# One branch for both halves of the first layer in the last group of a mixture of experts, the second layer behind it

## The chip, the core and the metric

The kernel runs on one core of a Trainium2 chip. A core has a matrix engine (TensorE, PE in the profile, with its weight loads as PEld), three engines for elementwise work (VectorE or DVE, ScalarE or ACT, GpSimd or POOL) and SyncE (SP), which issues DMA transfers. Each engine has its own instruction queue and waits for the others by semaphores. The metric is the time of the whole program on the device in microseconds, lower is better. Each time is the median of several runs.

## The reference

The reference is attention in a linear form with random features (8 batches, 8 heads, sequence 576, head size 64, 128 features), whose output becomes 4608 tokens of 512 numbers, and on them a mixture of experts in which each token goes to one of 8 experts. Cut to what matters here:

```python
q_p, k_p = (phi(q_s), phi(k_s))                 # 128 random features, exp
num = np.einsum('bhsm,bhmd->bhsd', q_p, kv)     # kv = sum over s of k_p * v
x = (num / den).transpose(0, 2, 1, 3).reshape(4608, 512)

e_idx = np.argmax(x @ w_gate, axis=1)           # one expert per token
gate_w = probs[np.arange(N), e_idx]
eom = 1.0 / (1.0 + np.exp(-(x @ w_output_gate)))
for e in range(8):
    mask = e_idx == e
    h = np.maximum(x[mask] @ w1[e], 0.0)        # 512 -> 1024
    ye = h @ w2[e]                              # 1024 -> 512
    out[mask] = gate_w[mask, None] * eom[mask, e, None] * ye
```

Inputs and outputs are float32.

## The kernel before

**Stages.** Attention runs as 32 units in four chunks of the tokens. Its output goes to a DRAM array (`rows`), token by token, and after each chunk a routing step counts the tokens of each expert. The expert work is cut into *items*: an item is up to 128 tokens of one expert. Items come in four groups of 8, 8, 9 and 24 slots, one group behind each chunk (`KS`); the last group holds whatever tokens are left, and its later slots stay empty. How many tokens an item has, which expert it uses, and whether the expert differs from that of the item before are known only at run time. They are read into registers of the engines, and the code of a step stands in `tc.If` branches on these registers: `regs[n, 0, ...]` says whether item n exists, `regs[n, 1, ...]` whether it begins a new expert, and in the last group `regs[n, "few", ...]` whether it has at most 64 tokens (`FEW`, half of `P` = 128).

**One item.** GpSimd gathers the token rows by an indirect DMA (`gx`), SyncE issues a DMA that transposes them (`xt`). All products are taken in fp16 as three terms of high and low parts (high by high, high by low, low by high). The first layer (`hidden`, L1373) runs in two halves of 512 hidden numbers: each half is 48 matmuls of 128x128 weights on the tokens into one PSUM bank (`ph`), with as many tokens as columns: 128 in the full arm, 64 in the small one. For each half ScalarE takes the relu (`relu`, L1388, into `hh`, the fp16 high part), then VectorE the remainder (`rest`, L1392, into `hl`); in the small arm two memsets follow that clear the unused lanes (L1397, L1398). The second layer (`second`, L1400) has for each half 12 matmuls with 512 columns, from `hh` and `hl` with the weights `w2h` and `w2l`, and both halves sum into one bank (`po`). ScalarE scales the result (`os`, L1456), and GpSimd scatters it to the output (`put`, L1445).

**A new expert.** SyncE loads its weights in float32 (`bring`, L1289). Each of the two layers' weights is split by quarters: ScalarE makes the fp16 high part (`swh`, L365), VectorE the low part (`swl`, L369), so eight splits on each of the two engines for one switch, inside a branch that is empty when the expert stays. A quarter of the new weights may be written only when TensorE has used the old one: `free` at L1333 names the step behind which this is so.

**What sets the order.** The order on each engine is fixed when the program is built. A planner (`Plan.order`, L173) lists all steps with their engine, an assumed duration, the steps that they come after, and a rank. It goes through time, and of the steps that can start within 0.1 us of the earliest (`TIE`) takes the one with the lowest rank. An expert switch counts with its full duration (0.95 us for a split on ScalarE, 1.14 on VectorE) only behind the items after which one is assumed (`ASSUMED`, in the last group items 26, 31 and 37), otherwise with 0.1. `early` makes a step count as done before its end, `lead` lets a step start that long before another one is done, or, if it is negative, that long after. PSUM's banks are given out there too: three banks (class `b`) are shared by the `ph` and `po` of all items.

**The steps that the change touches.** In the first three groups an item has four steps on TensorE: `hA` and `hB` (the two halves of the first layer) and two steps `out`. In the last group (`joint`) before the change it has three: `hA`, a branch with the first half; `hB`, one branch with the second half and the first part of the second layer (`hidden_and_second`); and `out` 1, the second part of the second layer, outside of the branch on the number of tokens. `either` (L1360) makes that branch: `tc.If` on `few` with the 64-token code first, `Else` with the 128-token code. ScalarE's relu and VectorE's remainder go through `either` too. In this run 38 items were executed; those of the last group are 25 to 37, and 25, 36 and 37 have at most 64 tokens.

Of the kernel before, what the change touches and what calls it, by code (L numbers as in the profile page):

```python
# [21 lines left out]
P = 128  # L22
# [3 lines left out]
DM = H * D  # L26
# [7 lines left out]
FC = F // P  # L34
# [15 lines left out]
NG = len(GROUPS)  # L50
# [206 lines left out]
def attention_moe(ctx: ExitStack, tc: tile.TileContext, kqt, kqn, v, om, wg, w1, w2, cf, cm, ci, out):  # L257
# [1009 lines left out]
    def item(n):  # L1267
# [45 lines left out]
        for w in (1, 2):  # L1313

            user = n - 1 if n <= ALT else n - 2
            before = cuts_of(user, w) if n != ALT and user >= 0 else []
            plan.add(
                ("bring", n, w), ("SP",), 1.8 if full and aside(n) else 0.4, lambda w=w: bring(w), rank=-900.0 + n,
                after=[flag_step[n, 1, ("SP",)]] + behind(n, w) + (before if n else [("w0l", w, x) for x in range(NQ)] if SPECULATE else []), dma=5.8 if full else 0.0,
                tiles=[b for b, _ in SPARE[w]] if n == ALT else [],  # L1320
            )
            if gr < FINE:
                last = [] if n == 0 else [("hB", n - 1)] if w == 1 else [("out", n - 1, 1)]
                plan.add(
                    ("sw", n, w), ("ACT", "DVE"), (3.8, 4.9) if full else (0.3, 0.3), lambda w=w: switch(w), rank=-1500.0 + n,
                    early=2.2 if full else None,
                    after=[flag_step[n, 1, ("ACT", "DVE")], ("bring", n, w)] + last,
                )
                continue
            for x in range(NQ):  # L1330
                half = x // (NQ // 2)
                joint = FEW > 0 and slots[n - 1][0] == NG - 1
                free = ("hB" if half else "hA", n - 1) if w == 1 else ("hB", n - 1) if joint and not half else ("out", n - 1, half)  # L1333
                plan.add(
                    ("swh", n, w, x), ("ACT",), 0.95 if full else 0.1, lambda w=w, x=x: cut(w, x, "ACT"),
                    after=[flag_step[n, 1, ("ACT",)], ("bring", n, w), free], rank=CUT + n,
                )
                plan.add(
                    ("swl", n, w, x), ("DVE",), 1.14 if full else 0.1, lambda w=w, x=x: cut(w, x, "DVE"),
                    after=[flag_step[n, 1, ("DVE",)], ("swh", n, w, x)], rank=CUT + n,  # L1340
                )
# [18 lines left out]
        def either(eng, fn):  # L1360

            if gr < NG - 1 or not FEW:
                return lambda: fn(P)

            def step():
                with tc.If(regs[n, "few", (eng,)] > 0) as small_block:
                    fn(FEW)
                with small_block.Else():
                    fn(P)

            return step

        def hidden(g, w_):  # L1373
# [16 lines left out]
        def rest(g, w_):  # L1390
# [5 lines left out]
            if w_ < P:  # L1396
                nc.vector.memset(hh(n)[:, sl, w_:], 0.0)  # L1397
                nc.vector.memset(hl(n)[:, sl, w_:], 0.0)  # L1398

        def second(g):  # L1400
            po = banks["po", n]
            for f in range(g * (FC // 2), (g + 1) * (FC // 2)):
# [2 lines left out]
                        po, x(n)[:, f, :], w[f // 2][:, f % 2, :], start=(f == 0 and a == 0), stop=(f == FC - 1 and a == 2)  # L1405
                    )


        joint = gr == NG - 1 and FEW > 0

        def hidden_and_second(w_):
            hidden(1, w_)
            second(0)

        for g in range(2):
            name = "hA" if g == 0 else "hB"
            both = joint and g
            add(
                (name, n), "PE", 5.2 if both else 2.6,
                either("PE", hidden_and_second if both else lambda w_, g=g: hidden(g, w_)),  # L1420
                tiles=[("xt", n), ("hh", n), ("hl", n)] if both else [("xt", n)],
                bank=[("b", ("ph", n, g), [FC // 2, P])] + ([("b", ("po", n), [DM])] if both else []),
                after=[("xt", n), *cuts_of(n, 1, halves_of[g])]
                + ([("hA", n)] if g else [("hB", n - 1)] if joint and slots[n - 1][0] == gr else [])
                + ([("rest", n, 0), *cuts_of(n, 2, halves_of[0])] if both else []),
                **(dict(early=2.6, lead={("rest", n, 0): 2.6, **{c: 2.6 for c in cuts_of(n, 2, halves_of[0])}}) if both else {}),
            )
            add(
                ("relu", n, g), "ACT", 0.48, either("ACT", lambda w_, g=g: relu(g, w_)), after=[(name, n)], rank=-600.0 + n,
                tiles=[("hh", n)],  # L1430
            )
            add(
                ("rest", n, g), "DVE", 0.6, either("DVE", lambda w_, g=g: rest(g, w_)), after=[("relu", n, g)], rank=-600.0 + n,
                tiles=[("hh", n), ("hl", n)], frees=[("ph", n, g)],
            )

        for g in range(1 if joint else 0, 2):
            add(
                ("out", n, g), "PE", 2.6, lambda g=g: second(g), rank=R + 5, tiles=[("hh", n), ("hl", n)],
                after=[("rest", n, g), *cuts_of(n, 2, halves_of[g])] + ([("hB" if joint else "out", n, *(() if joint else (0,)))] if g else []),  # L1440
                bank=None if g else ("b", ("po", n), [DM]),
            )

# [97 lines left out]
```

## Time and profile before

| what | value |
|---|---|
| runs | 699.62, 702.99, 706.42 us (median 702.99) |
| the profiled execution's own time | 703.85 us |
| its span, first to last instruction | 702.1 us |
| mean granted TensorE clock | 0.951 |
| busy TensorE matmuls, of the span | 615.9 us (88%) |
| busy VectorE, ScalarE, GpSimd | 472.8, 372.0, 330.2 us |
| last group's matmuls | 552.1 to 689.2, 137.1 us |
| TensorE busy in them | 132.4 us, at a granted clock of 1.00 |
| from the last matmul's stretch to the end | 12.9 us |

The profile is of one execution, so stretches of it are set against its own 703.85 us, and not against the median. A row of a timeline is the start in us from the beginning of the span, the duration, the engine, the source line, the operation, output and input with their shapes, and in square brackets how long the engine had been idle and what ended that. Rows of TensorE show a matmul longer than the distance to the next one, since matmuls overlap. A row with `PEldq COMPARE_BRANCH` lists branch instructions in TensorE's queue: their count, their least, median and greatest duration in ns, and when the first and the last began.

### The profile page before, as it was taken

The page shows a single profiled execution, that of the slowest core. Times are in us where ns is not written, and L with a number is a line of the kernel's source. Part 1 is how long each engine was busy: PE and PEld are TensorE (multiplying, and loading weights), DVE is VectorE, ACT ScalarE, POOL GpSimd, SP SyncE. Part 2 cuts the span into 40 slices and gives each one's busy share as a digit, 9 for nine tenths or more (in the row PEclk, how much of TensorE's full clock was granted, in tenths as well). Part 3 has the DMA queues.
Part 4 walks back from the last instruction along what each step waited for, and adds up shares of the span by engine and source line. Part 5 has one row for each costly group of instructions (what it writes and reads, how often), then busy time and mean ns, then how long its engine had stood idle before and what let it go on. Part 6 is the DMA issues. An engine that isn't in the chain of part 4 may idle for free. (4 is left out here: it accounts for less than half of the span.)

```text
span 702.1 us, 22897 instructions
## 1 busy us (share of the span) xinstructions
PE 615.9 (88%) x8763; PEld 474.6 (68%) x8763; DVE 472.8 (67%) x1300; ACT 372.0 (53%) x869; POOL 330.2 (47%) x207
## 2 busy tenths in 40 slices
PE   6999974899989987989989877899999999999982
PEld 6889863766766765766767646677777576676751
DVE  5997888977797897778899977763465431341160
ACT  5967883776586546666866425652341431331150
POOL 1323353668757857858489546666121121131210
PEclk9999986899999998999999967989999999999997
DMA  8565887999999939798899584639864934722730
GB/s 295 213 153 162 277 243 204 205 271 250 300 251 299 266 95 249 207 266 284 226 280 214 125 195 95 110 74 212 298 154 118 263 87 133 265 78 66 255 104 8
DMA packets 181031, 137.76 MB, mean 196 GB/s; under 512 B 139535, under 2 KB 162575, under 8 KB 179600
## 3 DMA queue, kind: packets, MB, share of 16 engines
q1 hardware_dynamic: 174800, 116.13, 65.0%
q0 software_dynamic: 6080, 19.72, 8.3%
q8 instruction: 83, 1.36, 0.8%
q14 instruction: 68, 0.56, 0.3%
HBM read 83.69 MB, written 19.69 MB: 147 GB/s over the span
## 5 line engine op out<-in xcount | busy, mean ns | idle before, releaser
L544 ACT ACTIVATE ef<-pp,nb 128x128 f32<-128x128 f32 x576 | 164.2, 388 | 118.8 <-DVE nb L538 87.5
L1381 PE MATMUL ph<-xt,w1h 128*128 128x128 f16 (+1 forms) x2432 | 209.4, 220 | 3.1 <-DMA xt<-gx 2.3
L1381 PE MATMUL ph<-xt,w1l 128*128 128x128 f16 (+1 forms) x1216 | 205.1, 220 | 1.1 <-DVE w1l L369 0.6
L1381 PEld LDWEIGHTS <-w1h 128*128 128x128 f16 x2432 | 184.2, 99 | 12.1 <-issue 3.0
L1392 DVE SCALAR_TENSOR_TENSOR hl<-ph,hh 128x512 f16<-128x512 f32 (+1 forms) x76 | 50.4, 665 | 123.3 <-ACTq L1310 78.7
L567 POOL TENSOR_TENSOR es<-ef,es 128x1152 f16<-128x1152 f32 x44 | 106.2, 2416 | 49.7 <-ACT es L565 28.2
L1381 PEld LDWEIGHTS <-w1l 128*128 128x128 f16 x1216 | 120.1, 100 | 0.9 <-DVE w1l L369 0.8
L1404 PE MATMUL po<-w2h,hh 128*128 128x512 f16 x304 | 116.4, 383 | 3.8 <-DVE hl L1398 2.1
L1404 PE MATMUL po<-w2h,hl 128*128 128x512 f16 x304 | 116.2, 382 | 1.0 <-DVE hl L1392 0.8
L1404 PE MATMUL po<-w2l,hh 128*128 128x512 f16 x304 | 116.2, 382 | 0.0
L1344 POOL DMA_INDIRECT gx<-rows,gi x38 | 40.9, 1076 | 153.6 <-ACT os L1456 108.6
L525 DVE TENSOR_REDUCE pp<-pp 128x3 f32<-128x384 f32 x192 | 102.1, 555 | 10.8 <-PE pp L503 9.8
L1404 PEld LDWEIGHTS <-hh 128*128 128x128 f16 x608 | 55.7, 98 | 67.6 <-issue 5.4
L1388 ACT ACTIVATE hh<-ph 128x512 f16<-128x512 f32 (+1 forms) x76 | 44.3, 585 | 93.7 <-PE ph L1381 88.4
L503 PE MATMUL pp<-omh,xhi 64*128 64x128 f16 x432 | 49.2, 232 | 28.0 <-ACT ef L544 9.8
L437 POOL TENSOR_TENSOR xlo<-xt,xhi 128x1152 f16<-128x1152 f32 x24 | 57.2, 2382 | 30.8 <-ACT xhi L430 8.3
L715 POOL TENSOR_TENSOR xs<-xf,xs 128x576 f16<-128x576 f32 x32 | 42.8, 1337 | 57.2 <-DVE xs L711 25.8
L503 PEld LDWEIGHTS <-xhi 64*128 64x128 f16 x864 | 37.9, 101 | 43.2 <-issue 18.0
L1456 ACT ACTIVATE os<-po,gx 128x512 f32<-128x512 f32 x38 | 26.1, 688 | 76.8 <-PE po L1404 63.9
L565 ACT CAST es<-ef 128x1152 f16<-128x1152 f32 x44 | 51.2, 1172 | 9.3 <-DMA et<-es 8.7
L1404 PEld LDWEIGHTS <-hl 128*128 128x128 f16 x304 | 29.9, 98 | 38.6 <-DVE hl L1392 2.4
L681 PE MATMUL pn<-kvs,et 128*128 128x65 f16 (+1 forms) x960 | 41.8, 199 | 11.6 <-DMA et<-es 5.9
(160 smaller groups left out, 1015.8 us busy)
## 6 DMA issues: line engine op xcount, KB each, us to landing
r<-w SPq DMA_DIRECT2D x10, 2048.0 KB
xt<-kqt SPq DMA_DIRECT2D x32, 576.0 KB
xn<-kqn SPq DMA_DIRECT2D x24, 576.0 KB
rawv<-v SPq DMA_DIRECT2D x32, 325.0 KB
rows<-xs SPq DMA_DIRECT2D x16, 576.0 KB
r<-w SPq DMA_DIRECT2D x8, 512.0 KB
ef<-w SPq DMA_DIRECT2D x2, 512.0 KB
et<-w SPq DMA_DIRECT2D x2, 512.0 KB
```

The source lines that it names most:

```text
L437: lambda t0=t0, t1=t1: nc.gpsimd.tensor_tensor(out=xl(u)[:, t0:t1], in0=xt32(u)[:, t0:t1], in1=xh(u)[:, t0:t1], op=ALU.subtract),
L503: nc.tensor.matmul(banks["pp", 2 * u + i, g][:, c, :], x[r, t], w[r, :], start=(a == 0), stop=(a == len(ops) - 1))
L525: nc.vector.tensor_reduce(out=pp[:, 3, 0:3], in_=pp[:, 0:3, :], op=ALU.min, axis=AX.X)
L544: nc.scalar.activation(ef(n)[:, c, :], banks["pp", n, g][:, c % 3, :], AF.Exp, bias=nb(n)[:, c : c + 1], scale=-SK)
L565: nc.scalar.copy(es(slot_es(n))[:, 0], ef(n))
L567: nc.gpsimd.tensor_tensor(out=es(slot_es(n))[:, 1], in0=ef(n), in1=es(slot_es(n))[:, 0], op=ALU.subtract)
L681: nc.tensor.matmul(pn[lo:hi, c - c0, :], a[:, c, lo:hi], w[:, b, :], start=(i == 0), stop=(i == len(ops) - 1))
L715: nc.gpsimd.tensor_tensor(out=x[:, :, P + o : P + o + D], in0=xf(pr)[:, :, o : o + D], in1=x[:, :, o : o + D], op=ALU.subtract)
L1381: nc.tensor.matmul(ph[:, f4, 0:w_], w[qd][:, kk, fo : fo + P], xt(n)[:, x, 0:w_], start=(a == 0), stop=(a == 3 * KC - 1))
L1388: nc.scalar.activation(hh(n)[:, sl, 0:w_], banks["ph", n, g][:, :, 0:w_], AF.Relu)
L1392: nc.vector.scalar_tensor_tensor(out=hl(n)[:, sl, 0:w_], in0=banks["ph", n, g][:, :, 0:w_], scalar=0.0, in1=hh(n)[:, sl, 0:w_], op0=ALU.ma ...
L1404: nc.tensor.matmul(po, x(n)[:, f, :], w[f // 2][:, f % 2, :], start=(f == 0 and a == 0), stop=(f == FC - 1 and a == 2))
```

## The change

In the last group the step `hA` is gone. One step `hB` now holds both halves of the first layer (`hidden_both`) in one branch, and on TensorE this branch has the 128-token code first and the 64-token code in the `Else` (`step_full_first`, on `few < 1`). ScalarE's and VectorE's branches stay as they were. The second layer's two parts are both steps `out` outside of the branch, as in the other groups.

For the planner the joint step costs 5.2 us and counts as done after 2.6 (`early`); the first relu comes after that, the second 2.6 us later (`lead` of -2.6). The joint step takes both `ph` banks at once and the first `out` takes `po`; before, `hA` took one `ph`, and `hB` took the other together with `po`. Quarters of the first layer's weights that belong to the second half may come 2.6 us later than the step's start. All four splits of a new expert's first-layer weights now wait for the joint step of the item before, where the first two waited for `hA`; the first two of the second layer wait for `out` 0, where they waited for `hB`. The three groups ahead are built as before.

```diff
--- before.py
+++ after.py
@@ -1330,7 +1330,7 @@
             for x in range(NQ):
                 half = x // (NQ // 2)
                 joint = FEW > 0 and slots[n - 1][0] == NG - 1
-                free = ("hB" if half else "hA", n - 1) if w == 1 else ("hB", n - 1) if joint and not half else ("out", n - 1, half)
+                free = ("hB" if half or joint else "hA", n - 1) if w == 1 else ("out", n - 1, half)
                 plan.add(
                     ("swh", n, w, x), ("ACT",), 0.95 if full else 0.1, lambda w=w, x=x: cut(w, x, "ACT"),
                     after=[flag_step[n, 1, ("ACT",)], ("bring", n, w), free], rank=CUT + n,
@@ -1367,6 +1367,15 @@
                     fn(FEW)
                 with small_block.Else():
                     fn(P)
+
+            def step_full_first():
+                with tc.If(regs[n, "few", (eng,)] < 1) as full_block:
+                    fn(P)
+                with full_block.Else():
+                    fn(FEW)
+
+            if eng == "PE":
+                return step_full_first
 
             return step
 
@@ -1397,6 +1406,37 @@
                 nc.vector.memset(hh(n)[:, sl, w_:], 0.0)
                 nc.vector.memset(hl(n)[:, sl, w_:], 0.0)
 
+
+        joint = gr == NG - 1 and FEW > 0
+
+        def hidden_both(w_):
+            hidden(0, w_)
+            hidden(1, w_)
+
+        if joint:
+            banks_ = [("b", ("ph", n, g), [FC // 2, P]) for g in range(2)]
+            add(
+                ("hB", n), "PE", 5.2, either("PE", hidden_both), tiles=[("xt", n)], bank=banks_, early=2.6,
+                after=[("xt", n), *cuts_of(n, 1)], lead={c: 2.6 for c in cuts_of(n, 1, halves_of[1])},
+            )
+        for g in range(2):
+            name = "hA" if g == 0 else "hB"
+            if not joint:
+                add(
+                    (name, n), "PE", 2.6, either("PE", lambda w_, g=g: hidden(g, w_)), tiles=[("xt", n)],
+                    bank=("b", ("ph", n, g), [FC // 2, P]),
+                    after=[("xt", n), *cuts_of(n, 1, halves_of[g])] + ([("hA", n)] if g else []),
+                )
+            add(
+                ("relu", n, g), "ACT", 0.48, either("ACT", lambda w_, g=g: relu(g, w_)), rank=-600.0 + n,
+                after=[("hB" if joint else name, n)] + ([("relu", n, 0)] if g else []), tiles=[("hh", n)],
+                lead={("hB", n): -2.6} if joint and g else {},
+            )
+            add(
+                ("rest", n, g), "DVE", 0.6, either("DVE", lambda w_, g=g: rest(g, w_)), after=[("relu", n, g)], rank=-600.0 + n,
+                tiles=[("hh", n), ("hl", n)], frees=[("ph", n, g)],
+            )
+
         def second(g):
             po = banks["po", n]
             for f in range(g * (FC // 2), (g + 1) * (FC // 2)):
@@ -1405,39 +1445,10 @@
                         po, x(n)[:, f, :], w[f // 2][:, f % 2, :], start=(f == 0 and a == 0), stop=(f == FC - 1 and a == 2)
                     )
 
-
-        joint = gr == NG - 1 and FEW > 0
-
-        def hidden_and_second(w_):
-            hidden(1, w_)
-            second(0)
-
         for g in range(2):
-            name = "hA" if g == 0 else "hB"
-            both = joint and g
-            add(
-                (name, n), "PE", 5.2 if both else 2.6,
-                either("PE", hidden_and_second if both else lambda w_, g=g: hidden(g, w_)),
-                tiles=[("xt", n), ("hh", n), ("hl", n)] if both else [("xt", n)],
-                bank=[("b", ("ph", n, g), [FC // 2, P])] + ([("b", ("po", n), [DM])] if both else []),
-                after=[("xt", n), *cuts_of(n, 1, halves_of[g])]
-                + ([("hA", n)] if g else [("hB", n - 1)] if joint and slots[n - 1][0] == gr else [])
-                + ([("rest", n, 0), *cuts_of(n, 2, halves_of[0])] if both else []),
-                **(dict(early=2.6, lead={("rest", n, 0): 2.6, **{c: 2.6 for c in cuts_of(n, 2, halves_of[0])}}) if both else {}),
-            )
-            add(
-                ("relu", n, g), "ACT", 0.48, either("ACT", lambda w_, g=g: relu(g, w_)), after=[(name, n)], rank=-600.0 + n,
-                tiles=[("hh", n)],
-            )
-            add(
-                ("rest", n, g), "DVE", 0.6, either("DVE", lambda w_, g=g: rest(g, w_)), after=[("relu", n, g)], rank=-600.0 + n,
-                tiles=[("hh", n), ("hl", n)], frees=[("ph", n, g)],
-            )
-
-        for g in range(1 if joint else 0, 2):
             add(
                 ("out", n, g), "PE", 2.6, lambda g=g: second(g), rank=R + 5, tiles=[("hh", n), ("hl", n)],
-                after=[("rest", n, g), *cuts_of(n, 2, halves_of[g])] + ([("hB" if joint else "out", n, *(() if joint else (0,)))] if g else []),
+                after=[("rest", n, g), *cuts_of(n, 2, halves_of[g])] + ([("out", n, 0)] if g else []),
                 bank=None if g else ("b", ("po", n), [DM]),
             )
 
```

## The prediction

> **What bounds the kernel now.** I read the page first, then the last group by stretch, then single items.
>
> ```profile
> span 702.1 us, 22897 instructions
> PE 615.9 (88%) x8763; PEld 474.6 (68%) x8763; DVE 472.8 (67%) x1300; ACT 372.0 (53%) x869; POOL 330.2 (47%) x207
> ```
>
> TensorE works for 88% of the span. The change touches only items of the last group (items 25 to 37 ran; 38 and later were skipped). The table of busy time by stretch, cut where each item's first matmul starts, shows them; columns are the stretch, its length, then busy time and count for PE, weight loads, DVE, ACT and POOL, then granted clock, DMA share and GB/s:
>
> ```profile
> core 0: us, PE busy (x) PEld busy (x) DVE busy (x) ACT busy (x) POOL busy (x), PEclk, DMA share, GB/s
> 552.10:562.49 10.39, 8.76 (x122) 5.32 (x121) 7.08 (x12) 8.11 (x10) 1.99 (x2) 1.00 0.79 263
> 562.49:573.05 10.56, 10.56 (x122) 7.64 (x120) 4.73 (x5) 2.83 (x5) 1.98 (x2) 1.00 0.34 82
> 573.05:583.78 10.73, 10.70 (x122) 7.72 (x121) 1.38 (x2) 1.88 (x3) 2.00 (x2) 1.00 0.31 84
> ...
> 605.26:616.59 11.33, 10.86 (x121) 7.65 (x120) 6.38 (x7) 7.96 (x10) 2.00 (x2) 1.00 0.47 105
> 616.59:627.13 10.54, 10.54 (x121) 7.71 (x120) 5.37 (x6) 3.15 (x5) 3.72 (x2) 1.00 0.30 79
> ...
> 659.40:670.17 10.77, 10.70 (x121) 7.72 (x120) 1.38 (x2) 1.88 (x3) 1.99 (x2) 1.00 0.96 399
> 670.17:679.01 8.84, 8.30 (x121) 5.14 (x120) 6.27 (x11) 7.61 (x10) 1.00 (x1) 1.00 0.26 69
> 679.01:689.20 10.19, 8.47 (x121) 5.18 (x119) 5.33 (x10) 2.75 (x5) 1.51 (x1) 1.00 0.05 16
> sum 137.10, PE 132.38 PEld 92.69 DVE 44.85 ACT 45.58 POOL 26.16; mean PE 10.18 PEld 7.13 DVE 3.45 ACT 3.51 POOL 2.01
> ```
>
> Items 25, 36 and 37 are small (64 lanes); the ten between are full. 132.38 of 137.10 us are matmuls at the full clock (1.00 in every row). The 4.72 us of idle are all that any rearrangement of the branches can win, plus about 0.2 us an item that the busy column hides: a full item takes 10.54 us at best (item 31), and 10.73 to 10.77 in items 27 and 35. Item 27 shows that 0.2:
>
> ```profile
> 577.07 0.60 ACT L1388 ACTIVATE hh<-ph 128x512 f16<-128x512 f32 x1 [3.08 <-PE ph L1381]
> 577.76 0.69 DVE L1392 SCALAR_TENSOR_TENSOR hl<-ph,hh 128x512 f16<-128x512 f32 x1 [7.45 <-ACTq L1310]
> 578.35 0.22 PE L1381 MATMUL ph<-xt,w1l 128*128 128x128 f16 x1
> 578.60 0.38 PE L1404 MATMUL po<-w2h,hh 128*128 128x512 f16 x1
> 578.61 0.60 ACT L1388 ACTIVATE hh<-ph 128x512 f16<-128x512 f32 x1 [0.94 <-PE ph L1381]
> 578.82 0.38 PE L1404 MATMUL po<-w2l,hh 128*128 128x512 f16 x1
> 579.30 0.69 DVE L1392 SCALAR_TENSOR_TENSOR hl<-ph,hh 128x512 f16<-128x512 f32 x1 [0.85 <-ACTq L1310]
> ```
>
> The first relu (577.07) and its remainder (577.76 to 578.45) are for the first half; a second-layer matmul takes a step of 0.22 (578.60 to 578.82), so 24 of them take 5.28 of the 10.54 us and 96 of the first layer 0.055 each. The second layer starts at 578.60 instead of 0.055 after 578.35, so 0.19 is lost to a remainder that ended late. ACT had waited for TensorE, not for itself.
>
> **The change part by part.** For an item that runs, TensorE's order stays the same: half A, half B of the first layer, then the second layer's halves, which I call S0 and S1. What changes is where the code lies. Before, A is one branch, and B with S0 another, each with the small arm first: 48 matmuls and 48 weight loads for A, 60 and 60 for B with S0. After, one branch holds A and B (192 instructions an arm), the full arm first, and S0 and S1 lie behind it once. TensorE executes the same matmuls and weight loads: 0.
>
> *One branch fewer.* The rows of TensorE's branch at its line, over the run, over items 26 to 35 and in items 25 and 36:
>
> ```profile
> L1366 PEldq COMPARE_BRANCH  x32: 65/264/3349, 549.0 to 683.9; - x32
> L1366 PEldq COMPARE_BRANCH  x19: 207/330/430, 564.2 to 661.5; - x19
> L1366 PEldq COMPARE_BRANCH  x2: 231/1790/3349, 556.4 to 560.0; - x2
> L1366 PEldq COMPARE_BRANCH  x1: 2231/2231/2231, 673.1 to 673.1; - x1
> ```
>
> In the full items a taken branch costs the sequencer 0.21 to 0.43 us, and item 27 has no gap on TensorE but the one at 578.60: the matmuls queued ahead hide the branch. Dropping one saves 0. The jump that stays moves from ahead of each half to between B and S0, where the sequencer waits for the first remainder anyway; 0.33 us fit, so 0.
>
> *Item 25.* The small arm of B with S0 ended with a jump over the other arm: the 3349 ns that begin at 556.4, so until 559.7.
>
> ```profile
> 556.48 0.38 PE L1404 MATMUL po<-w2h,hh 128*128 128x512 f16 x1
> 558.92 0.17 DVE L1398 MEMSET hl<- 128x128 uint32 x1
> 559.90 0.38 PE L1404 MATMUL po<-w2h,hh 128*128 128x512 f16 x1 [0.67 <-ACT w1h L365]
> ```
>
> S0 began at 556.48 and S1 at 559.90, where 12 steps would have ended S0 at 559.12. The view blames ACT, but the branch covers that time. After, the small arm lies second and falls through to S0: no jump. S1 then waits for the remainder, whose last memset ends at 559.09; with 0.14 from a remainder's end to the matmul (613.85 to 614.00, below) it starts at 559.23: 0.67 won. The small items pay instead a jump over the full arm on entry. Nothing shows a jump over 193 instructions; the nearest is over 122: from 0.21 to 3.35 us. Queued ahead of it are up to 12 matmuls of the previous S1, 2.6 us, so 0 to 0.75 exposed for each of items 25 and 36. I take 0, by the 19 rows of which none exceeds 0.43; item 37 is covered below.
>
> Also in item 25, the small B arm ran dry without any wait:
>
> ```profile
> 555.34 0.22 PE L1381 MATMUL ph<-xt,w1h 128*128 128x64 f16 x2 [0.44 <-issue]
> 556.08 0.19 PE L1381 MATMUL ph<-xt,w1l 128*128 128x64 f16 x1 [0.51 <-issue]
> ```
>
> I cannot name its cause; it stays (0), with 1.0 won or lost as ends.
>
> *Items 36 and 37, A to B.* Here the branches between the halves do show, since a 64-lane matmul lasts 0.03 us:
>
> ```profile
> 671.54 0.19 PE L1381 MATMUL ph<-xt,w1l 128*128 128x64 f16 x1
> 671.79 0.22 PE L1381 MATMUL ph<-xt,w1h 128*128 128x64 f16 x2
> ```
>
> 671.54 to 671.79 less one step: 0.22 won in item 36. The same in item 37 wins nothing: its S0 waits for VectorE, which works off the last expert switch until then (four second-layer splits from 678.55, then the remainder at 683.09):
>
> ```profile
> 678.55 4.62 DVE L369 SCALAR_TENSOR_TENSOR w2l<-r,w2h 128x1024 f16<-128x1024 f32 x4
> 683.09 0.41 DVE L1392 SCALAR_TENSOR_TENSOR hl<-ph,hh 128x256 f16<-128x256 f32 x1
> 683.79 0.38 PE L1404 MATMUL po<-w2h,hh 128*128 128x512 f16 x1 [1.58 <-DVE hl L1398]
> ```
>
> *Order on ACT and DVE at an expert switch.* All four splits of the next expert's first-layer weights are now freed by the joint step, which the planner counts as done after 2.6 of its 5.2 us; the second relu is due at 5.2. So ACT gets the third split (0.95 by the planner) ahead of that relu, where it had two. On chip, at the switch behind item 30:
>
> ```profile
> 611.71 0.59 ACT L1388 ACTIVATE hh<-ph 128x512 f16<-128x512 f32 x1
> 612.18 2.00 ACT L365 ACTIVATE w1h<-r 128x1024 f16<-128x1024 f32 x2
> 610.90 2.36 DVE L369 SCALAR_TENSOR_TENSOR w1l<-r,w1h 128x1024 f16<-128x1024 f32 x2 [0.19 <-ACT w1h L365]
> 613.17 0.68 DVE L1392 SCALAR_TENSOR_TENSOR hl<-ph,hh 128x512 f16<-128x512 f32 x1
> 614.00 0.38 PE L1404 MATMUL po<-w2h,hh 128*128 128x512 f16 x1 [0.40 <-DVE hl L1392]
> ```
>
> One split later (1.00) the relu ends at 613.30 instead of 612.30, the remainder starts near 613.40 instead of 613.17: 0.23 lost. In items 25 and 36 VectorE's first two splits hide it. On DVE the planner sees the third split's remainder at 6.69 and this one at 6.79, exactly its tie of 0.1; if it falls the other way, S1 waits one split more (2.36/2): 1.2 lost in each of items 25 and 30, 0 in 36, where VectorE's chain decides later anyway. I take the order as it is and keep 2.4 as an end. Without a switch the splits are skipped and nothing waits.
>
> *PSUM.* The joint step takes two of three banks at once; they are freed by the previous item's second remainder (579.99 in item 27), long before the next item's 583.78: 0.
>
> Sum: -0.67 - 0.22 + 0.23 = -0.66 us. The profiled execution took 703.85 us (span 702.1), 0.86 above the median 702.99 of the runs. 702.99 - 0.66 = **702.3 us**. The runs lie from 699.62 to 706.42, so a median can move by some 2 us by itself.
>
> **The rivals.**
>
> *The long jump is not hidden (slower).* The ten full items now jump over 193 instructions between B and S0. When item 25's branch began, about 30 instructions were queued (S0's 24 and the end of B); as many of the first layer are 15 matmuls of 0.055, 0.83 us. With the 0.19 that S0 waits anyway, a branch over 1.02 us shows. At 2.23 each ten of them cost 12 us: **714**; at 3.35, 23. For it: two branches in the small items took that long. Against it: 19 of 19 in the full items took at most 0.43. The small ones ran through their arm at 0.03 us a matmul, twice as fast as the full arm's code is used up. [...] Chance 0.10.
>
> *The first relu is released by the whole branch (slower).* A and B now share a branch. If ACT were let go only when B ends, S0 would wait as S1 does in item 27's rows: relu at 578.61, remainder to 579.99, S0 at 580.13 instead of 578.60, 1.53 in each of ten items: **718**. Against: item 27's second relu started at 578.61 although S0, in the same branch, had only just begun. For: the first relu is already late, 1.18 us after the end of A (575.89, 48 steps after 573.05). Decided at a delay of 1.4. Chance 0.08.
>
> *Everything closes (faster).* The late remainder (eight items, 0.2 each: 1.6), item 25's dry spell (1.0) and the terms above: -0.67 - 0.22 - 2.6 = -3.5, **699.5**. For: without the branch between A and B, TensorE's release of ACT may come on time, as in item 31. Against: no row ties the delay to that branch. Chance 0.12.
>
> **How the numbers follow.** Forecast 0.70, the rivals 0.10, 0.08 and 0.12. A measurement of this kernel tells about 1% (7 us) from no change. The closing rival stays below that by itself and reaches it only with the scatter: faster 0.05. The two slower ones lie beyond it, less the part of the first in which only a few jumps stall, plus a little scatter: slower 0.14. Same: 0.81. The range runs from 697 (closing rival and 2.5 of scatter) to 709 (2.4 for the planner's tie, 1.5 for the entry jumps, 1.0 for the dry spell, 2 of scatter); about 0.17 is left out, most of it above.
>
> **What would show it.** S1 of item 25 within 0.2 us of its last memset, and no gap between the halves of item 36, confirm the two gains. Full items of 10.7 us with a branch of at most 0.43 between B and S0 confirm the zeros; a branch over 1 us there, or items of 12 us, show the first rival, and a first relu that starts with B's end the second. Items of 10.54 throughout show the third. ACT's third split ahead of the second relu in item 30 shows the order.

## The result, and the profile after

Over 20 runs of each kernel the changed one took 707.92 us (median; 702.31 to 715.37), the kernel before 701.16 us: a ratio of 1.0101, with a 95% interval of 1.0069 to 1.0133. That is 7.1 us slower (1.01% of 701.16), and the interval leaves no room for no change, where the forecast was 0.7 us faster, no measurable change; the time itself lies within the stated 697 to 709. Two later comparisons gave 1.0198 (1.0132 to 1.0264) and 1.0153 (1.0078 to 1.0228).

The first profile of the changed kernel shows the loss although its span happens to be short. First its page's head, then the table by stretch, the rows of items 25, 27, 29, 30, 35 and 36, in the columns of the prediction's table:

```profile
span 700.7 us, 22895 instructions
PE 612.5 (87%) x8763; PEld 471.8 (67%) x8763; DVE 467.8 (67%) x1300; ACT 371.7 (53%) x869; POOL 332.5 (47%) x207
```

```profile
545.98:555.74 9.76, 8.14 (x121) 5.07 (x121) 7.41 (x12) 7.68 (x10) 1.99 (x2) 1.00 0.80 275
566.28:576.82 10.54, 10.54 (x122) 7.71 (x120) 1.38 (x2) 1.88 (x3) 2.00 (x2) 1.00 0.36 79
587.36:600.73 13.37, 10.71 (x122) 7.63 (x120) 1.38 (x2) 1.88 (x3) 2.00 (x2) 1.00 0.92 342
600.73:612.06 11.33, 10.70 (x121) 7.63 (x120) 7.52 (x8) 8.48 (x10) 2.00 (x2) 1.00 0.38 77
654.47:668.83 14.36, 12.39 (x122) 8.22 (x120) 1.39 (x2) 1.88 (x3) 2.00 (x2) 0.88 0.98 334
668.83:678.81 9.98, 8.14 (x122) 5.07 (x121) 7.41 (x12) 8.17 (x10) 1.00 (x1) 1.00 0.09 31
```

TensorE runs the same 8763 matmuls. Items 29 and 35 stick out: 13.37 and 14.36 us where the other full items take 10.5 to 11.3. The last two columns tell them apart: while they ran, DMA was 92% and 98% busy, at over 330 GB/s. These are the weight loads for the switches at items 31 and 37 (without them, in no_loads, the two items show 75 and 78 GB/s). (New experts begin at items 26, 31 and 37 here; their weights are split while the items ahead, 25, 30 and 36, run.)

Two profiles from different batches don't subtract well: the attention part alone moved the start of item 25 between 546 and 557 us. So both kernels were run again side by side on one chip (labels before_again and after_third). The kernel before there, the rows of items 25, 27, 29, 30, 35, 36 and 37, then the whole group in one row:

```profile
549.51:559.08 9.57, 8.50 (x122) 5.28 (x120) 6.28 (x11) 7.67 (x10) 2.00 (x2) 1.00 0.83 279
569.82:580.59 10.77, 10.69 (x121) 7.72 (x120) 1.38 (x2) 1.88 (x3) 2.00 (x2) 1.00 0.29 80
591.32:602.07 10.75, 10.70 (x121) 7.72 (x120) 1.38 (x2) 1.88 (x3) 2.00 (x2) 1.00 0.98 410
602.07:613.40 11.33, 10.86 (x122) 7.65 (x120) 6.39 (x7) 7.96 (x10) 2.00 (x2) 1.00 0.45 103
656.21:666.99 10.78, 10.71 (x122) 7.72 (x120) 1.38 (x2) 1.88 (x3) 2.00 (x2) 1.00 0.97 401
666.99:675.83 8.84, 8.30 (x121) 5.14 (x120) 6.27 (x11) 7.46 (x10) 1.01 (x1) 1.00 0.34 74
675.83:685.67 9.84, 8.18 (x121) 5.18 (x119) 5.33 (x10) 3.02 (x5) 1.24 (x1) 1.00 0.05 16
549.51:685.67 136.16, 132.02 (x1561) 92.61 (x1559) 44.77 (x62) 45.53 (x63) 25.95 (x24) 1.00 0.49 147
```

The changed kernel on the same chip, the same items, and item 32 ahead of item 35:

```profile
552.62:564.22 11.60, 8.79 (x121) 5.31 (x122) 7.42 (x12) 7.65 (x10) 1.99 (x2) 1.00 0.84 259
574.75:585.50 10.75, 10.71 (x122) 7.73 (x121) 1.38 (x2) 1.88 (x3) 2.00 (x2) 1.00 0.37 77
596.22:611.47 15.25, 12.55 (x121) 8.07 (x120) 1.38 (x2) 1.88 (x3) 1.99 (x2) 0.89 0.88 295
611.47:623.90 12.43, 10.86 (x121) 7.65 (x120) 7.53 (x8) 8.48 (x10) 2.00 (x2) 1.00 0.32 67
634.44:645.54 11.10, 10.70 (x122) 7.72 (x120) 1.38 (x2) 1.88 (x3) 2.00 (x2) 1.00 0.36 76
667.05:681.00 13.95, 10.86 (x122) 7.70 (x120) 1.38 (x2) 2.14 (x4) 1.99 (x2) 1.00 0.90 330
681.00:691.57 10.57, 8.47 (x120) 5.20 (x121) 7.41 (x12) 7.92 (x10) 1.00 (x1) 1.00 0.10 33
691.57:700.27 8.70, 8.02 (x121) 5.12 (x119) 4.20 (x9) 2.30 (x5) 1.72 (x1) 1.00 0.05 15
552.62:700.27 147.65, 134.15 (x1560) 93.08 (x1560) 44.95 (x62) 45.45 (x63) 26.06 (x24) 0.99 0.48 136
```

The group is 11.5 us longer (147.65 less 136.16), and the clock time of this comparison agrees: 1.53% of 702.67 is 10.8 us. By items there are two parts. Items 29, 35 and 32 lose 4.50, 3.17 and 0.34 (item 32 took 10.76 in the kernel before): 8.0 us. The items ahead of a switch, 25, 30 and 36, lose 2.03, 1.10 and 1.73, of which item 37 gives 1.14 back: 3.7 us. The other full items are equal within about 0.2.

Not all of these 3.7 us is a matter of the order at the switches. In items 25 and 36 the first relu itself starts later than in the kernel before. These are its rows in item 25, of before_again and then of after_third:

```profile
552.10 0.38 ACT L1388 ACTIVATE hh<-ph 128x256 f16<-128x256 f32 x1 [1.65 <-PE ph L1381]
556.10 0.38 ACT L1397 ACTIVATE hh<-ph 128x256 f16<-128x256 f32 x1 [3.26 <-remote]
```

That is 2.59 us behind the item's start in the one and 3.48 in the other, though the second half of the first layer begins 1.40 us behind it in both. In item 36 it is 1.65 and 2.25.

What a stall looks like, in item 29 of the changed kernel on that chip (TensorE's timeline, then its branch rows in this item and in item 35):

```profile
605.02 0.39 PE L1444 MATMUL po<-w2h,hl 128*128 128x512 f16 x1 [2.67 <-DVEq L1310]
605.25 0.41 PE L1444 MATMUL po<-w2h,hh 128*128 128x512 f16 x1
605.47 0.62 PE L1444 MATMUL po<-w2l,hh 128*128 128x512 f16 x1
605.88 0.63 PE L1444 MATMUL po<-w2h,hl 128*128 128x512 f16 x1
```

```profile
L1372 PEldq COMPARE_BRANCH  x2: 73/128/184, 600.6 to 607.0; - x2
L1372 PEldq COMPARE_BRANCH  x2: 3317/3747/4177, 671.4 to 676.8; - x2
```

In item 29 TensorE stops for 2.67 us after the second matmul of S0. The row blames a branch in VectorE's queue, but VectorE's two instructions for this item fill only 1.38 us, and the same stop in the first profile is put down to "issue". The branch itself was short there (184 ns): the jump landed in code that had arrived, and TensorE stopped two matmuls on. In item 35 the branch itself took 3317 ns. After the stop of item 29 the steps grow from 0.22 to 0.43 us (605.47 to 605.88, and for 3.4 us on), and the granted clock of the stretch is 0.89: the stop was followed by half the clock, which cost another 1.7 us. The stop of 2.74 us in item 35 here brought no half clock (1.00), while one of 1.97 in the first profile did (0.88). So these stops alone don't tell when the half clock comes.

What was TensorE waiting for? Queue q8 of the DMA view carries instructions, in packets of 16 KB. That these are TensorE's is inferred from how its long branches line up with them. In the first profile the branch of item 35 ran from 658.85 to 661.45; DMA in that stretch, two of its queue rows:

```profile
q1 hardware_dynamic: 75, 0.97, 88.2%
q8 instruction: 1, 0.02, 2.3%
```

One code packet went through among 0.97 MB on q1, which carries the weight loads. The trace has it from 659.08 to 660.05, so the branch ended 1.40 us after its packet. Long branches of other traces end as long after theirs: the two of the kernel before 1.38 (559.73 after 558.35) and 1.43 (675.28 after 673.85), item 35 in after_third 1.38, item 29 in two_branches 1.35, item 35 in shift220 1.51. The stops in straight code end in the same way: in item 29 TensorE went on 1.34 us after its packet (605.02 after 603.68) and in the first profile 1.44 (595.97 after 594.53). Two branches do not fit: the jump into the small arm at item 36 ended 2.4 us after its packet in after_third, and 3.0 in after_again.

### The profile page after: what moved, and what is told of

Same layout as the page of the kernel before. It is cut to its first block, busy times and chain, and to the rows that moved or that the text cites. A ratio compares the mean times of both kernels' runs of the same rounds, so it can differ in the third digit from the quotient of the medians.

```text
span 700.7 us, 22895 instructions
## 1 busy us (share of the span) xinstructions
PE 612.5 (87%) x8763; PEld 471.8 (67%) x8763; DVE 467.8 (67%) x1300; ACT 371.7 (53%) x869; POOL 332.5 (47%) x207
## 5 line engine op out<-in xcount | busy, mean ns | idle before, releaser
L503 PE MATMUL pp<-omh,xhi 64*128 64x128 f16 x432 | 48.1, 227 | 28.1 <-ACT ef L544 10.4
## 6 DMA issues: line engine op xcount, KB each, us to landing
r<-w SPq DMA_DIRECT2D x10, 2048.0 KB, 11.3
```

The costliest lines, as they stand in the source:

```text
L503: nc.tensor.matmul(banks["pp", 2 * u + i, g][:, c, :], x[r, t], w[r, :], start=(a == 0), stop=(a == len(ops) - 1))
```

## The experiments

The theory of the late code, from the first profiles: TensorE's code comes in the packets of 16 KB (83 of them, 1.36 MB in the profile before), a packet's worth of code is a block, and a jump over 193 instructions leaves too little work to cover the wait for the next block when a block's limit lies shortly ahead of it, above all under the weight loads. No row shows when a block is asked for. Up to the last group the two first profiles have 252 to 255 recorded instructions of TensorE a packet (14336 on 57 packets in the one after, 14305 on 56 in the one before). While items 26 to 35 ran, 17 packets came in in after_third and 18 in the first profile, for some 4320 instructions (two arms of 192 and 48 of the second layer an item): 240 to 254 a packet. In item 29 TensorE stopped in straight code, four instructions behind the jump's target (two matmuls with their weight loads); taken as a limit, that place puts the one before it 55 to 58 instructions ahead of the jump. With 436 instructions of code an item (the 432, two branches and two semaphore waits) the same distance is 91 to 103 in item 32 and 124 to 151 in item 35 (an estimate from these counts and 252 to 255 a packet). There the target lies beyond the next limit, and there the branch itself was long (3317 ns in item 35, and 1.06 us in item 32 of the first profile).

**The changed kernel again, the order, and moved limits.** No edit in the first. In the second the splits wait for the second relu and remainder:

```diff
-after=[flag_step[n, 1, ("ACT",)], ("bring", n, w), free], rank=CUT + n,
+after=[..., free] + ([("relu", n - 1, 1)] if joint and w == 1 and half else []), rank=CUT + n,
-after=[flag_step[n, 1, ("DVE",)], ("swh", n, w, x)], rank=CUT + n,
+after=[..., ("swh", n, w, x)] + ([("rest", n - 1, 1)] if joint and w == 1 and half else []), rank=CUT + n,
```

In the third, 116 instructions that never run (56 matmuls with their weight loads, in a branch that is never taken) move what follows (the fourth has both edits):

```diff
+def never():
+    for _ in range(56):
+        nc.tensor.matmul(banks["ph", n, 0][:, 0, 0:FEW], w1h[0][:, 0, 0:P], xt(n)[:, 0, 0:FEW], start=True, stop=True)
 def step_full_first():
+    if i == 0:
+        with tc.If(regs[n, "few", (eng,)] > 1):
+            never()
     with tc.If(regs[n, "few", (eng,)] < 1) as full_block:
```

> The changed kernel once more, unchanged. [...] Then the stalls come back at the same two items, 29 (13.4 us instead of 10.5) and 35 (14.4), since both are bound to places in the code and to the loads for the switches at items 31 and 37; last group 141 to 143 us; ratio 1.007 to 1.013. Rival, a stall by chance: they stand at other items or are missing.

> The changed kernel, with the third and fourth split of the next expert's first-layer weights held back behind the second relu (ScalarE) and the second remainder (VectorE), as in the kernel before. Theory that the order at the switches costs the time: the second part of the second layer starts 1.1 us earlier in items 25 and 36 and 0.8 us earlier in item 30, the last group loses 2 to 3 us (item 37 takes 1.1 of them back, since VectorE's splits decide there), ratio 1.006. Theory of the late code: that is all, items 29 and 35 still take 13 and 14 us. If the order were the whole loss, the ratio would be 1.000.

> [...] Theory of the late code: the block limit now falls ahead of the full arm or into the jumped part in items 29 and 35, so both take 10.5 to 11.1 us instead of 13.4 and 14.4; item 27 or 30 may lose up to 0.5 us; the last group takes 135 to 137 us and the ratio is 1.000 to 1.003. Rival, the jump itself or the weight loads hold TensorE up by data: 29 and 35 stay at 13 to 14 us, ratio 1.010.

> The two edits together: 116 instructions that are never run, and the second relu ahead of the third split. Both theories together: last group 133 to 135 us, ratio 0.996 to 1.000. If the order costs nothing by itself: 135 to 137 us, as with the shifted code alone.

| kernel | item 29 | item 35 | group | ratio (95%) |
|---|---|---|---|---|
| after_again | 15.18 | 14.38 | 147.24 | 1.0198 (1.0132 to 1.0264) |
| relu_first | 14.78 | 14.75 | 145.68 | 1.0111 (1.0056 to 1.0166) |
| shift116 | 10.73 | 11.14 | 140.59 | 1.0025 (0.9986 to 1.0064) |
| both116 | 10.72 | 11.13 | 138.07 | 1.0070 (1.0028 to 1.0112) |

The stalls came back at the same two items, and code that never runs took them away. The sizes were missed: after_again and relu_first lost more than expected (1.007 to 1.013, and 1.006), and both116 did not reach its 0.996 to 1.000 and 133 to 135 us. In shift116 items 27, 29 and 35:

```profile
573.55:585.31 11.76, 10.70 (x122) 7.73 (x121) 1.38 (x2) 1.88 (x3) 2.00 (x2) 1.00 0.36 72
596.04:606.77 10.73, 10.71 (x122) 7.72 (x121) 1.38 (x2) 1.88 (x3) 2.00 (x2) 1.00 0.93 377
662.23:673.37 11.14, 10.70 (x122) 7.79 (x121) 1.38 (x2) 1.88 (x3) 2.00 (x2) 1.00 0.90 363
```

Items 29 and 35 run under the same weight loads (0.93 and 0.90) without a stall; item 27 now has one, of 1.0 instead of the 0.5 expected, and the group was 140.6 instead of 135 to 137, since items 25 and 30 still took 11.6 and 12.7, by the order and the late first relu. The order by itself gave 1.6 us: items 25 and 30 took 1.2 and 1.1 less, and item 36's 0.4 was more than taken back by item 37 (1.1), whose second layer waits for VectorE anyway. The profiles put both116 ahead of shift116 by 2.5 us, while the timed runs put it behind, within intervals that overlap; 0.4% is more than these runs can order.

**What makes the code late.** In the first no weights are fetched for the last two switches (this kernel and the next have one timed run, and only their profiles are read), in the second the unused code is 220 instructions, in the third TensorE has no small arm, in the fourth the small arm comes first:

```diff
-nc.sync.dma_start(r1 if which == 1 else r2, ...)
+if n < ALT + 2:
+    nc.sync.dma_start(r1 if which == 1 else r2, ...)
```

```diff
-    for _ in range(56):
+    for _ in range(108):
```

```diff
-    return step_full_first
+    return lambda: fn(P)
```

```diff
-if eng == "PE":
-    return step_full_first
```

> The changed kernel without the weight loads for the switches at items 31 and 37: those experts are computed from weights that were in place, so part of the outputs is of the wrong expert; all other work stays. [...] Rival, the jump over 193 instructions costs by itself: 29 and 35 stay at 13 to 15 us.

> As the kernel with 116 unused instructions, but with 220 of them (108 matmuls and their weight loads). Theory of the late code: in item 29 the block limit now falls close to the end of the full arm, and the next one is far: 10.5 to 11.0 us. In item 35 it falls 80 instructions ahead of the jump, and the weights of the next expert come in: 13 to 15 us, with a branch of 2 to 3.5 us between the first and the second layer. Rival, both items are slow for the data they wait for: both 13 to 15 us, as in the changed kernel; rival, any unused code helps: both 10.5 to 11.

> The changed kernel without the small arm on TensorE: every item of the last group runs the first layer on all 128 lanes, with no branch on the number of tokens there. Theory of the late code: without a jump no stall, items 26 to 35 take 10.5 to 10.8 us each (item 30 11.3 to 12.4, by the order on ScalarE and VectorE); items 25, 36 and 37 take 1.5 to 2.7 us more each for 96 matmuls at 0.056 instead of 0.028; last group 139 to 143 us, ratio 1.003 to 1.010. Rival, the stalls have nothing to do with the jump: 29 and 35 at 13 to 15 us, last group 146 to 150, ratio 1.015 to 1.02.

> The changed kernel with the 64-lane code first on TensorE too, as in the kernel before: the full items jump over 193 instructions on entry instead of between the two layers. Theory of the late code: the distance matters, not the place. By the block limits, item 29 is free (10.5 to 11), item 35 still loses 1.5 to 4, items 31 and 34 lose 0.5 to 1.5 each inside the first layer; last group 139 to 145, ratio 1.004 to 1.012. Rival, the order of the arms is what costs: no item over 11.3 except 25, last group 137, ratio 1.000.

Items 29 and 35 in no_loads, in shift220, and in one_arm:

```profile
594.56:605.79 11.23, 10.87 (x121) 7.65 (x120) 1.38 (x2) 1.88 (x3) 1.99 (x2) 1.00 0.32 75
661.31:672.48 11.17, 10.70 (x121) 7.78 (x120) 1.38 (x2) 1.88 (x3) 1.99 (x2) 1.00 0.38 78
```

```profile
596.36:607.14 10.78, 10.70 (x121) 7.72 (x120) 1.38 (x2) 1.88 (x3) 1.99 (x2) 1.00 0.98 407
661.51:678.22 16.71, 13.62 (x122) 8.45 (x121) 1.38 (x2) 1.88 (x3) 1.99 (x2) 0.80 0.70 276
```

```profile
595.80:606.61 10.81, 10.70 (x121) 7.72 (x120) 1.38 (x2) 1.88 (x3) 2.00 (x2) 1.00 0.96 394
662.16:673.35 11.19, 10.70 (x121) 7.79 (x120) 1.38 (x2) 1.88 (x3) 1.99 (x2) 1.00 0.88 362
```

Without the weight loads (75 and 78 GB/s) both items are down to 11.2 with the jump still there: the jump alone is not the cause. Item 29 was expected at most at 11.3; a stop of 0.4 us is left there at the same matmul. Item 35 was expected at 10.5 to 10.8; its second layer starts 0.4 us late in one_arm too, which has no jump, so this rest need not be the jump's, and its cause is open. With 220 instructions item 29 is free and item 35 worse than ever, as placed beforehand (16.71 against 13 to 15 expected; its branch took 3711 ns, and half clock followed for 6.8 us). Without a jump neither stalls although the loads run. In one_arm the stalls are gone and the gain with them: the small items take 12.3, 11.3 and 10.4 us, the group 143.66, the ratio is 1.0110 (1.0052 to 1.0167), the last two a little over what was expected. Taking the small arm out also moves the limits, so that the jump is needed rests on ten full items of which none stalled. So the stalls of 2.7 us took all three here: skipped code, a block limit in the wrong place, and the weight loads. Without the weight loads smaller ones are left, up to the 1.0 us of item 27 in shift116 (72 GB/s).

small_first came out at 1.0102 (1.0058 to 1.0146), group 145.46, as expected in sum, but by luck, since the items were others. Items 25, 30 and 35 of it:

```profile
554.06:568.53 14.47, 11.09 (x121) 5.95 (x120) 8.34 (x12) 8.32 (x10) 1.99 (x2) 0.76 0.66 204
611.53:626.51 14.98, 10.88 (x122) 7.63 (x121) 7.53 (x8) 8.49 (x10) 2.00 (x2) 1.00 0.57 104
669.55:680.84 11.29, 10.70 (x121) 7.75 (x120) 1.38 (x2) 1.88 (x3) 2.00 (x2) 1.00 0.88 360
```

Items 31 and 34 lost nothing, item 35 only 0.8 in its first layer, and items 25 and 30 stalled by 2.5 and 3.5 us, which had not been expected; they went on 1.35 and 1.30 us after a code packet. A jump taken on entry is taken while up to 12 slow matmuls of the second layer are still queued, by estimate 2.6 us of work (12 steps of 0.22) against 0.8 us behind the first layer (the prediction's 30 instructions). In sum that gained nothing here.

**The kernel before, and forms between.** Two branches for the two halves with the second layer outside (joint is off, the first splits freed by hA again); the kernel before with 165 unused instructions; the kernel before with the full arm first on TensorE; and both edits of above with 146 instructions. In the second edit `begun` is a list that marks the first use, and `never` is as above with 81 matmuls:

```diff
-joint = gr == NG - 1 and FEW > 0
+joint = False
-free = ("hB" if half or joint else "hA", n - 1) if w == 1 else ("out", n - 1, half)
+free = ("hB" if half else "hA", n - 1) if w == 1 else ("out", n - 1, half)
```

```diff
+first = eng == "PE" and i == 0 and not begun
 def step():
+    if first:
+        with tc.If(regs[n, "few", (eng,)] > 1):
+            never()
     with tc.If(regs[n, "few", (eng,)] > 0) as small_block:
```

```diff
+def step_full_first():
+    with tc.If(regs[n, "few", (eng,)] < 1) as full_block:
+        fn(P)
+    with full_block.Else():
+        fn(FEW)
+if eng == "PE":
+    return step_full_first
 return step
```

```diff
-    for _ in range(56):
+    for _ in range(71):
```

> The changed kernel with the two halves of the first layer again in a branch each (full arm first, second layer outside, the splits freed as in the kernel before). Theory of the late code: two jumps over 97 instructions within one block take as much of it away as one over 193: item 29 still loses 1.5 to 3 us (and up to 1.7 more at half clock), item 35 0.4 to 2; last group 139 to 144 us, ratio 1.004 to 1.012. Rival, it is the joint branch that stalls: no item over 11.3 but 25, last group 136 to 137.5, ratio 1.000.

> The kernel before with 165 instructions that are never run ahead of item 25 in TensorE's code. Its jumps over the small arms are taken while the slow second layer of the item before is still queued, and each is followed by 96 or 120 instructions. Theory of the late code: moved block limits can cost it little even during the weight loads: item 29 up to 0.8 us, item 35 0.5 to 1.5 (and up to 1.7 at half clock), the others nothing; last group 137 to 140.5 us, ratio 1.001 to 1.006. Rival, where the limits fall decides in this kernel too: 13 us or more in 29 and 35. Rival, this form never stalls: 136.5 to 137.

> The kernel before with the 128-lane code first in both of TensorE's branches, and nothing else. Theory of the late code: the jumps come behind the first layer's first half and behind the first part of the second layer, with 96 to 120 instructions between: no item from 26 to 35 over 11.4 us (item 30 11.3); item 25 starts the second part of its second layer 0.7 us earlier, since its arm no longer ends with a jump; last group 135.5 to 137 us, ratio 0.997 to 1.003. Rival, the arm order is what stalls: 29 and 35 at 13 us or more, ratio 1.008.

> As the kernel with 116 unused instructions and the second relu ahead of the third split, with 146 unused instructions. Theory of the late code: item 27's stall goes (11.4 to 10.8), item 34 gains one of up to 0.5; last group 137 to 138 us, so the ratio is 1.000 to 1.005, no better than the kernel before.

| kernel | item 29 | item 35 | item 36 | group | ratio (95%) |
|---|---|---|---|---|---|
| two_branches | 15.09 | 12.44 | 9.37 | 139.38 | 1.0067 (1.0022 to 1.0111) |
| before_shift165 | 10.54 | 12.06 | 8.84 | 135.39 | 1.0026 (0.9981 to 1.0072) |
| before_full_first | 10.54 | 10.54 | 11.91 | 135.21 | 1.0050 (1.0013 to 1.0086) |
| both146 | 10.54 | 10.65 | 11.40 | 135.46 | 1.0046 (1.0006 to 1.0086) |

two_branches still stalls in item 29, by a branch of 3680 ns: joining the halves is not needed for it, two short jumps close together did the same with the limits as they fall there. The kernel before, with its limits moved, loses 1.5 us in item 35 (TensorE went on 1.38 us after a code packet) and nothing in item 29. So it is not free of the stall; at this one place of the limits it lost less. Items 29 and 35 of before_shift165:

```profile
590.12:600.66 10.54, 10.54 (x121) 7.70 (x120) 1.39 (x2) 1.88 (x3) 2.00 (x2) 1.00 0.99 403
653.36:665.42 12.06, 10.70 (x121) 7.75 (x120) 1.38 (x2) 1.88 (x3) 1.99 (x2) 1.00 0.84 350
```

before_full_first has no stall in the full items, but item 36 took 11.91, over two gaps of 1.80 and 1.54 us put down to "issue" inside its small arms; they ended 1.5 and 1.3 us after a code packet. Its ratio had been expected at 0.997 to 1.003. In this batch the first relu was on time (see below), and the groups are near or below the shortest that was expected. None of the versions beats the kernel before.

**Side by side.** Both kernels unchanged, on one chip.

> The kernel before, unchanged, beside the changed kernel on the same chip. Theory that the late first relu belongs to the chip or the loading and not to the kernel: it is late in all full items but 26 and 31 (10.7 us each) or in none (10.5), and the same in the changed kernel. Where it is on time the last group takes 133 to 135 us, where it is late 136 to 137.5. Items 29 and 35 at most 10.8 either way. Rival, the joint branch brings the relu on time: late here, on time in the changed kernel.

> The changed kernel, unchanged, beside the kernel before. Theory of the late code: items 29 and 35 at 13 to 15.5 us; last group 6.5 to 10.5 us longer than that of the kernel before on this chip (141 to 142 where the first relu is on time, 145 to 148 where it is late); ratio 1.008 to 1.018.

Their rows stand above: before_again had a ratio of 0.9998 (0.9959 to 1.0038) to the other runs of the kernel before, after_third 1.0153. The group of after_third is 11.5 us longer, more than the 6.5 to 10.5 expected. Item 27 takes 10.77 in the one and 10.75 in the other, and its first relu starts 1.1 us late in both. So in the full items the late relu is not a matter of the branches. In the first profile of the changed kernel, and in all four profiles of the batch with two_branches, two of them forms of the kernel before, item 27 took 10.54. Within each batch on one chip the profiles agree in this. What makes it late stays open.

## Why the prediction was wrong

The steps in its own order:

- *TensorE does the same work.* Right: 8763 matmuls, and a full item with neither a stall nor a switch behind it takes as long as before within about 0.2 us.
- *The jump that stays costs 0, since 19 of 19 branches in the full items took at most 0.43 us.* This step failed, and with 8.0 of 11.5 us side by side it is most of the loss. The 19 rows were taken as the price of a jump. By the runs they are that only while the code at the target has arrived: the same jump took 0.18 to 0.34 us in most full items (first profile) and 3317 ns in item 35 (after_third), where it ended 1.38 us after its packet. The 3349 and 2231 ns of the small items, which the text set aside as a matter of faster arms, look like the same wait: each ended 1.4 us after a code packet.
- *The first rival*, a long jump that is not hidden, had this loss in it, at 0.10. It was priced as ten stalls of 1.2 us (714). The runs show two stalls of 2.7 us, half clock after one of them, and a small one in item 32. The rival's price lacked two things: the weight loads, without which the stop of item 29 came down to 0.4 us (no_loads), and the half clock behind a stop, 1.7 us in item 29 of after_third.
- *Item 25, 0.67 won.* S1 did start as the last memset ended (553.15 in the first profile), so the condition held, and the memset itself was late. VectorE took three splits ahead of that remainder instead of two. The item was 0.6 us shorter in the first profile, which lacks the dry spell (9.76 against 10.39), and 2.0 longer side by side, 0.9 of it by the later first relu.
- *The order on ACT and DVE, 0.23 lost in item 30.* This term was mis-sized. ScalarE's third split went ahead of the second relu, as forecast, and VectorE's remainder behind three splits, which was held as an end (1.2 us in each of items 25 and 30) and not taken. Taking the order back (relu_first against after_again) won 1.18 and 1.13 us in these two items, so the end was the right size, and 1.6 over the group. In items 25 and 36 the order was priced at 0; in 36 it cost 0.4, and item 37 gave back 1.1. The rest of the 3.7 us goes with the later first relu: in relu_first it starts 0.8 and 1.0 us later in items 25 and 36 than in before_again, and the two items are longer by the same (10.38 against 9.57, 9.80 against 8.84). The sum had no such term, and what delays that relu stays open.

The switch behind item 30, in the timeline of before_again and then of after_third (ScalarE, VectorE, and TensorE's S1):

```profile
606.62 2.00 ACT L365 ACTIVATE w1h<-r 128x1024 f16<-128x1024 f32 x2
608.52 0.59 ACT L1388 ACTIVATE hh<-ph 128x512 f16<-128x512 f32 x1
607.70 2.36 DVE L369 SCALAR_TENSOR_TENSOR w1l<-r,w1h 128x1024 f16<-128x1024 f32 x2 [0.19 <-ACT w1h L365]
609.98 0.68 DVE L1392 SCALAR_TENSOR_TENSOR hl<-ph,hh 128x512 f16<-128x512 f32 x1
610.81 0.38 PE L1404 MATMUL po<-w2h,hh 128*128 128x512 f16 x1 [0.40 <-DVE hl L1392]
```

```profile
615.99 2.94 ACT L365 ACTIVATE w1h<-r 128x1024 f16<-128x1024 f32 x3
618.83 0.58 ACT L1397 ACTIVATE hh<-ph 128x512 f16<-128x512 f32 x1
617.07 3.50 DVE L369 SCALAR_TENSOR_TENSOR w1l<-r,w1h 128x1024 f16<-128x1024 f32 x3 [0.19 <-ACT w1h L365]
620.48 0.68 DVE L1401 SCALAR_TENSOR_TENSOR hl<-ph,hh 128x512 f16<-128x512 f32 x1
621.31 0.38 PE L1444 MATMUL po<-w2h,hh 128*128 128x512 f16 x1 [1.54 <-ACT w2h L365]
```

Three splits instead of two on both engines put S1 9.84 us behind the item's start instead of 8.74.

- *Item 36, 0.22 won between the halves.* The gap did go in the first profile; the late S1 took more than it gave, and side by side so did the later first relu.
- *The second rival*, a first relu held to the branch's end, is out: the relu starts before the second half ends in every full item.
- *The third rival*, everything closes: the first profile alone looked like it. Side by side the late relu stays, so what closed there was not the change's doing.
- *The list of what would show it* named the branch's duration and items of 12 us. By the branch alone item 29 would have been missed, whose branch took 184 ns; its length told.

## What to carry to other kernels

A branch that skips code had no fixed price here: the same jump took from 0.18 to 3.7 us. Ask how much work TensorE still has when it needs code from the next block, and who else fills the DMA queues then. Moving the jump behind slow matmuls that are still queued was no cure here (small_first, 1.0102). If a stall sits at fixed items and carries "issue" or an engine that had long been done as its cause, put some never-executed instructions ahead: if the stall moves to another item, as from items 29 and 35 to 27 in shift116, it is the place of the code. And freeing an engine's steps earlier in a planner can let them pass the step that the bound engine waits for.

## What the runs showed of the hardware

- TensorE went on 1.3 to 1.5 us after the end of a code packet in the branches and stops listed above, and 2.4 and 3.0 us after it in two.
- The same jump over 193 instructions took 0.18 to 0.34 us in most full items, 1.06 in item 32 of the first profile and 2.04 in item 27 of shift116 while no weights came in (78 and 72 GB/s), and 2.60, 3.32 and 3.71 in item 35 of the first profile, after_third and shift220, under loads of 276 to 334 GB/s.
- Stops of TensorE of 2.0 to 3.1 us were followed by half clock in some cases, for 3.4 us or, in shift220 and small_first, 6.8, and not in others (0.89 in item 29 and 1.00 in item 35 of after_third; 1.00 behind 3.5 us in item 30 of small_first).
- In the full items TensorE's release of the first relu was 1.1 us late in most items in some batches and in none in others, for both kernels alike (item 27: 10.77 and 10.75 us side by side, 10.54 in the batch with two_branches).
